# Moving the last query block's product with V behind the second logits, in the last of four attention segments

## Chip, cores and metric

The kernel runs on one core of a Trainium2 chip. The metric is the device time of one execution in microseconds (us); lower is better. Every run told of here was at a granted TensorE clock of 1.0. Executions of one kernel lie within about 0.5 us of each other.

## The reference

A residual block in two halves: attention with a compressive memory, then a gated MLP with a spatial mix. Only the first half matters here. For each of 32 heads of 32 columns, in four segments of 512 tokens:

```python
for s in range(4):
    qs, ks, vs = q[:, :, s], k[:, :, s], v[:, :, s]
    logits = einsum('bhqd,bhkd->bhqk', qs, ks) * scale + mask      # causal
    p = softmax(logits)
    a_dot = einsum('bhqk,bhkd->bhqd', p, vs)                       # "the product with V"
    a_mem = (phi(qs) @ M) / (phi(qs) @ z + 1e-06)                  # memory of earlier segments
    outs.append(g * a_mem + (1 - g) * a_dot)
    M = M + phi(ks)^T @ vs                                         # state update
    z = z + sum(phi(ks))
```

After the last segment nobody reads M and z, so the kernel leaves that state update out.

## The kernel before

The kernel records instructions for each engine in program order, and a tracker adds the semaphore waits. It tracks SBUF in cells of 32 bytes and PSUM in whole banks (2 KiB). A wait means: this bank or cell is still being read or written by another engine.

PSUM has 8 banks. Banks 0 to 3 hold the logits of four heads, 4 and 5 the product with V (`PVA`), and 6 and 7 rotate for projections and state. A *group* `n` is four heads of one segment: 8 groups a segment, 32 in all, and the last segment has groups 24 to 31.

```python
def logits(n, rnd):                       # rnd 0, 1, 2: first, second, third logits
    parts = {0: ((0, 0, 512),), 1: ((1, 0, 384), (3, 384, 128)), 2: ((2, 0, 256),)}[rnd]
    wid = (512, 512, 256)[rnd]
    e = E[n % 2][rnd]
    for j, o, w in parts:
        for i in range(4):                # four heads, four 32-row tiles of the array
            pe.matmul(PS[:, i, o:o + w], qk[...], qk[...], ..., tile_position=(32 * i, 0))
    if rnd == 2 and n >= NQ:
        mem(n)                            # phi(q) @ M, reads MZB[:, c]
    act.activation(e[:, :, 0:wid], PS[:, 0:4, 0:wid], ACTF.Exp, scale=float(SCALE))
    # ... causal mask on GpSimd; for rnd 2 the memory's normalisation

def pv(n):                                # product with V: 4 query blocks, 40 matmuls
    c = n % NQ
    for cq in range(4):
        for j in range(cq + 1):
            rnd, o = {0: (0, cq * 128), 1: (1, cq * 128 - 128), 2: (2, cq * 128 - 256), 3: (1, 384)}[j]
            for i in range(4):
                pe.matmul(PVA[:, cq, i, :], E[n % 2][rnd][:, i, o:o + 128], V[:, j, 4 * c + i, 0:33],
                          start=(cq % 2 == 0 and j == 0 and i == 0), stop=False, ...)
    norm(n)                               # VectorE: divide by the row sums, add the memory part

def state(n):
    s, c = divmod(n, NQ)
    if s == NSEG - 1:
        return                            # nothing in the last segment
    b = next_bank()
    for tcl in range(4):
        pe.matmul(PS[:, b, 0:132], PK[n % 3][:, tcl, :], V[:, tcl, 4 * c:4 * c + 4, 0:33], ...)
    # ... VectorE: MSUM += bank, then MZB[:, c] = MSUM * mask
```

The order within a group:

```python
    logits(n, 0)
    fill(f1)                  # K projection of group n + 1: 8 matmuls of 512 columns
    if n > 0:
        pv(n - 1)
    logits(n, 1)
    if n > 0:
        state(n - 1)
    bg_pop()
    fill(f2)                  # Q projection of group n + 1: 8 matmuls of 512 columns
    logits(n, 2)
    # ... fill(f3), fill(f4): V or output projections
```

All three rounds of logits write the same four banks. So the second logits must wait for the exp of the first, and the third for the exp of the second. What stands between them on TensorE decides whether it stops.

The softmax here doesn't subtract the row's maximum and nothing guards it: scores larger than these inputs give would overflow.

Of the kernel before, what the change touches and what calls it, by code (L numbers as in the profile page):

```python
# [14 lines left out]
NSEG = 4  # L15
# [242 lines left out]
def bass_sequential_preLN__memory_aug_infini_attn__mixer_gmlp__prompt_kernel(  # L258
# [123 lines left out]
    def x_load(tc):  # L382
        sp.dma_start(XCH[tc % 4][:], x2d[tc * 128:(tc + 1) * 128, :])

    def wcols(ap, lo, hi):
        return ap[:, lo:hi].rearrange("(c p) n -> p c n", p=128)
# [29 lines left out]
    def mask_g():  # L416
        dve.tensor_copy(MASKG[:, :, :, 0:32],
                        GS[:].rearrange("p (c i) -> p c i", i=4).unsqueeze(3).to_broadcast([128, NQ, 4, 32]))
        for i in range(4):
            dve.tensor_single_scalar(MASKG[:, :, i, 0:32], MASKG[:, :, i, 0:32], BLK[:, i:i + 1], ALU.mult)  # L420
        for c in range(NQ):
            dve.tensor_copy(MASKG[:, c, :, 32], BLK[:])
# [24 lines left out]
    def to_T(dst, tcl, src):  # L447
        sp.dma_start_transpose(dst[:, :, tcl * 128:(tcl + 1) * 128], src[:])
# [40 lines left out]
    def phi_exp(n):  # L489
        q, p, e = phi_views(n)  # L490
        act.activation(e, q, ACTF.Exp)

    def phi_max(n):
        q, p, e = phi_views(n)
        dve.tensor_single_scalar(p, q, 1.0, ALU.add)
        dve.tensor_single_scalar(e, e, 1.0, ALU.min)
        dve.tensor_tensor(p, p, e, ALU.max)
        if n // NQ < NSEG - 1:
            sp.dma_start_transpose(PK[n % 3][:], PQK[n % 2][:, 1, :])


    def logits(n, rnd):
        qk = QK[n % 2]
# [5 lines that stand above are left out]
                pe.matmul(PS[:, i, o:o + w], qk[32 * i:32 * (i + 1), 1, j * 128:(j + 1) * 128],  # L509
                          qk[32 * i:32 * (i + 1), 0, j * 128:512], start=True, stop=True,  # L510
                          tile_position=(32 * i, 0))
        if rnd == 2 and n >= NQ:
            mem(n)
        act.activation(e[:, :, 0:wid], PS[:, 0:4, 0:wid], ACTF.Exp, scale=float(SCALE))
        for j, o, w in parts:
            d = e[:, :, o:o + 128]
            pool.affine_select(out=d, in_=d, pattern=[[0, 4], [1, 128]], compare_op=ALU.is_ge, fill=0.0,
                               base=0, channel_multiplier=-1)
        if rnd == 2 and n >= NQ:
            mem_norm(n)  # L520

    def pv(n):
        c = n % NQ
        for cq in range(4):
            for j in range(cq + 1):
                rnd, o = {0: (0, cq * 128), 1: (1, cq * 128 - 128), 2: (2, cq * 128 - 256), 3: (1, 384)}[j]
                for i in range(4):
                    pe.matmul(PVA[:, cq, i, :], E[n % 2][rnd][:, i, o:o + 128], V[:, j, 4 * c + i, 0:33],
                              start=(cq % 2 == 0 and j == 0 and i == 0), stop=False, skip_group_check=True)
        norm(n)  # L530

    def mem(n):
        c = n % NQ
        for cq in range(4):
            pe.matmul(PS[:, cq, 256:388], PQK[n % 2][:, 0, cq * 128:(cq + 1) * 128], MZB[:, c, :, 0:33],
                      start=True, stop=True)

    def mem_norm(n):
        om = PS[:, 0:4, 256:388].rearrange("p q (i d) -> p q i d", d=33)
        dve.tensor_single_scalar(RDM[:], om[:, :, :, 32], float(MEM_EPS), ALU.add)  # L540
        dve.reciprocal(RDM[:], RDM[:])
        dve.tensor_tensor(TM[n % 2][:], om[:, :, :, 0:32], RDM[:].unsqueeze(3).to_broadcast([128, 4, 4, 32]), ALU.mult)

    def norm(n):
        s, c = divmod(n, NQ)
        ot = OTOK[s % 2][:, :, c * 128:(c + 1) * 128].rearrange("p q (i d) -> p q i d", d=32)
        dve.reciprocal(RD[:], PVA[:, :, :, 32])
        dve.tensor_tensor(RD[:], RD[:], OMG[:, c:c + 1, :].to_broadcast([128, 4, 4]), ALU.mult)
        rb = RD[:].unsqueeze(3).to_broadcast([128, 4, 4, 32])
        if s == 0:  # L550
            dve.tensor_tensor(ot, PVA[:, :, :, 0:32], rb, ALU.mult)
        else:
            dve.tensor_tensor(TA[:], PVA[:, :, :, 0:32], rb, ALU.mult)
            dve.tensor_tensor(ot, TA[:], TM[n % 2][:], ALU.add)
        if c == NQ - 1:
            for tcl in range(4):
                to_T(OT, tcl, OTOK[s % 2][:, tcl, :])
# [4 lines that stand above are left out]
            return  # L562
        b = next_bank()
        for tcl in range(4):
            pe.matmul(PS[:, b, 0:132], PK[n % 3][:, tcl, :], V[:, tcl, 4 * c:4 * c + 4, 0:33],
                      start=(tcl == 0), stop=(tcl == 3))
        if s == 0:
            dve.tensor_copy(MSUM[:, c, :], PS[:, b, 0:132])
        else:
            dve.tensor_tensor(MSUM[:, c, :], MSUM[:, c, :], PS[:, b, 0:132], ALU.add)  # L570
        dve.tensor_tensor(MZB[:, c, :, 0:33], MSUM[:, c, :].rearrange("p (i d) -> p i d", d=33), MASKG[:, c, :, :],
                          ALU.mult)


    def xr_load(tc):
        sp.dma_start(XR[tc % 2][:], x2d[tc * 128:(tc + 1) * 128, :])
# [15 lines left out]
    def ln_tasks(src, dst, tcl):  # L592
        lnq[0].append((src, dst, tcl))

    def bg_pop():
        if lnq[2]:
            src, dst, tcl, k = lnq[2].pop(0)
            to_T(dst, tcl, ln_apply(src, k))
        if lnq[1]:
            it = lnq[1].pop(0)  # L600
            ln_rstd(it[3])
            lnq[2].append(it)
        if lnq[0]:
            it = lnq[0].pop(0)
            lnq[1].append(it + (ln_stats(it[0]),))
# [68 lines left out]
    def z2_gelu(k, tc, src):  # L674
        act.activation(Z2[:, tc, k * 448:(k + 1) * 448], src, ACTF.Gelu_apprx_tanh)
        zs.append((k, tc))
# [16 lines left out]
    for n in range(LAST + 1):  # L693
        s, c = divmod(n, NQ)
        f1, f2, f3, f4 = [], [], [], []
        if n < LAST:
            f1, f2 = [("qk", n + 1, 1)], [("qk", n + 1, 0)]
        if s == 0:
            f3 = [("v", 0, c, 1)] if c < 4 else [("v", 1, c - 4, 0)]
        elif s < NSEG - 1:  # L700
            if c < 2:
                f3, f4 = [("v", s, 2 * c, 1)], [("v", s, 2 * c + 1, 1)]
            elif c < 6:
                f3, f4 = [("wo", s - 1, c - 2, 0)], [("wo", s - 1, c - 2, 1)]
            else:
                f3, f4 = [("v", s + 1, 2 * (c - 6), 0)], [("v", s + 1, 2 * (c - 6) + 1, 0)]
        elif c < 2:
            f3, f4 = [("v", s, 2 * c, 1)], [("v", s, 2 * c + 1, 1)]
        elif c < 6:
            f3, f4 = [("wo", s - 1, c - 2, 0)], [("wo", s - 1, c - 2, 1)]  # L710
        elif c == 6:
            f3, f4 = [("z2", 0, 4, 0)], [("z2", 0, 5, 1)]
        else:
            f1, f2 = [("z2", 0, 6, 2)], [("z2", 0, 7, 3)]
            f3, f4 = [("z2", 0, 0)], [("z2", 0, 1)]

        def fill(lst):
            for u in lst:
                {"v": proj_v, "wo": wo, "qk": proj_qk, "z2": z2_group}[u[0]](*u[1:])

        if s < NSEG - 1 and c < 4:
            ln_tasks(XCH[c], XNT[(s + 1) % 2], c)
        if s < NSEG - 2 and c >= 4:
            x_load(4 * (s + 2) + c - 4)
        if s > 0 and c == 1:
            xr_load(4 * (s - 1))

        logits(n, 0)
        fill(f1)
        if n > 0:  # L730
            pv(n - 1)
        logits(n, 1)
        if n > 0:
            state(n - 1)
        bg_pop()
        fill(f2)
        logits(n, 2)
        if n == 0:
            mask_g()
        if n < LAST:  # L740
            phi_exp(n + 1)
        while n == LAST and staged:
            z2_gelu(*staged.pop(0))
        fill(f3)
        if n < LAST:
            phi_max(n + 1)
        bg_pop()
        fill(f4)
        bg_pop()
        if n == 1:  # L750
            sp.dma_start(WO[:], wcols(A_wo, 0, D))
        if n in (24, 26):
            win_load((n - 24) // 2)
    pv(LAST)
    xr_load(4 * (NSEG - 1))

# [98 lines left out]
```

## Time and profile before

| | before |
|---|---|
| time, median of 3 runs | 805.35 us (805.32 to 805.37) |
| span of the profiled run | 803.7 us |
| TensorE busy | 795.0 us, 99% |
| TensorE waits in the last segment | 1.3 us in the list, 7 times |

The profile page of the kernel before, its busy times and its chain of waits (the work that ended last, traced back):

```profile
span 803.7 us, 12539 instructions
...
PE 795.0 (99%) x5407; PEld 384.0 (48%) x5407; DVE 367.8 (46%) x756; ACT 302.7 (38%) x360; POOL 120.5 (15%) x234
...
PE 94%; DVE 2%; ACT 2%; DMA 0%; issue 0%
```

TensorE (PE) is the engine to relieve. Everything else is under half busy. With the same instructions, a gain can come only from TensorE's gaps.

The timeline of the kernel before, part of group 28 (start, duration, engine, operation with output and inputs, count, and in brackets the idle time in front and what ended it; TensorE's rows, with ScalarE's row of the second exp put among them, and other rows left out):

```profile
283.84 0.40 PE L209 MATMUL ps<-qk_102 32*128 32x512 bf16 x4
284.17 1.90 PE L209 MATMUL ps<-xnT_78,wk 128*128 128x512 bf16 x8
...
286.82 0.25 PE L209 MATMUL ps<-v,e_110 128*128 128x33 bf16 x4
287.01 0.40 PE L209 MATMUL ps<-qk_102 32*128 32x384 bf16 x8
287.34 1.90 PE L209 MATMUL ps<-xnT_78,wq 128*128 128x512 bf16 x8
...
287.46 1.88 ACT L209 ACTIVATE e_113<-ps 128x2048 bf16<-128x2048 f32 x1 [0.75 <-PE ps L209]
...
289.39 0.29 PE L209 MATMUL ps<-qk_102 32*128 32x256 bf16 x4 [0.15 <-ACT e_113 L209]
```

Read it from the end. The third logits (289.39) follow the exp of the second (287.46 + 1.88 = 289.34) by 0.05 us. The Q projection started at 287.34, and eight such matmuls are done well before. The bracket says 0.15 us, but the starts say more: from this projection to the third logits is 2.05 us, while the K projection hands over to the product with V after 1.74 us. (That hand-over has no change of tile shape. With one it takes about 1.83 us without a stop, as is worked out below, so the stop is 0.22 us and not the whole difference.) A matmul's end is modelled and overlaps the next start, so the bracket counts a stop too small.

The list of waits of TensorE, kernel before, from 240 to 320 us (total us, times, longest):

```profile
PE ps L209 <- ACT e_113 L209: 0.8, 4, 0.4
PE ps L209 <- ACT e_110 L209: 0.5, 3, 0.2
```

Seven stops, all on the second exp. And the chain of waits in order of time, kernel before, 276 to 310 us:

```profile
279.83 7.61 PE ps L209 x84
287.43 0.02 issue
287.46 1.89 ACT e_113 L209
289.34 0.05 issue
289.39 7.59 PE ps L209 x84
```

Once in each group the critical path leaves TensorE for ScalarE's exp and comes back.

### The profile page before, as it was taken

What the parts mean: (1) busy time and instruction counts of PE and PEld (TensorE: products, weight loads), DVE (VectorE), ACT (ScalarE), POOL (GpSimd) and SP (SyncE); (2) the same over time, 40 slices, a digit from 0 to 9 for tenths busy, and PEclk for the clock granted to TensorE, in tenths of its full rate; (3) what the DMA queues carried; (4) which work ended last, traced back from release to release, by engine and by line L of the source; (5) the groups of instructions that cost most, each with busy time, mean ns of one, the idle gap of its engine ahead of it and who ended that gap; (6) DMA issues with size and microseconds to landing.
All of it is one profiled execution on the core that took longest, in us unless ns stands there. A gap on an engine that the chain in (4) does not pass through costs nothing.

```text
span 803.7 us, 12539 instructions
## 1 busy us (share of the span) xinstructions
PE 795.0 (99%) x5407; PEld 384.0 (48%) x5407; DVE 367.8 (46%) x756; ACT 302.7 (38%) x360; POOL 120.5 (15%) x234
## 2 busy tenths in 40 slices
PE   8999999999999999999999999999999999999998
PEld 4445544455554445455544444444444444444444
DVE  4653688669854675844563000054234324423332
ACT  3888876887787666133333333100000000000000
POOL 2342333233322331100131000000000000000000
PEclk9999999999999999999999999999999999999999
DMA  9682544454425323621116000550270044011002
GB/s 296 157 172 60 92 80 119 80 99 81 93 47 126 113 54 68 189 60 53 53 53 131 1 1 0 193 115 1 79 138 1 26 106 85 1 59 53 1 7 86
DMA packets 125992, 64.79 MB, mean 81 GB/s; under 512 B 94832, under 2 KB 114928, under 8 KB 125936
## 3 DMA queue, kind: packets, MB, share of 16 engines
q1 hardware_dynamic: 125936, 63.99, 33.9%
q8 instruction: 42, 0.69, 0.3%
q14 instruction: 14, 0.11, 0.1%
HBM read 32.51 MB, written 8.39 MB: 51 GB/s over the span
## 4 chain that ended last, share of the span: by engine, by line
PE 94%; DVE 2%; ACT 2%; DMA 0%; issue 0%
PE ps L209 94%; ACT e_113 L209 1%; ACT e_110 L209 1%; DMA xch_97<-in_A_x_dram 0%; DVE stats_61 L209 0%; DVE stats_62 L209 0%; ACT e_109 L209 0%; DVE stats_59 L209 0%; DVE ta L209 0%; DVE otok_120 L209 0%; DVE hch_86 L209 0%; DVE stats_60 L209 0%; DVE pqk_104 L209 0%; DVE lno_90 L209 0%; DVE rd L209 0%
## 5 line engine op out<-in xcount | busy, mean ns | idle before, releaser
L209 PE MATMUL ps<-w_out,yT 128*128 128x512 bf16 (+1 forms) x462 | 97.4, 373 | 0.0
L209 PE MATMUL ps<-wspT_127,z_124 128*128 128x512 bf16 x448 | 97.0, 379 | 0.0
L209 PE MATMUL ps<-wspT_126,z_124 128*128 128x512 bf16 x448 | 97.0, 379 | 0.0
L209 PEld LDWEIGHTS ps<-w_out,yT 128*128 128x128 bf16 x462 | 45.2, 98 | 51.7
L209 PEld LDWEIGHTS ps<-wspT_126,z_124 128*128 128x128 bf16 x448 | 43.8, 98 | 52.9
L209 PEld LDWEIGHTS ps<-wspT_127,z_124 128*128 128x128 bf16 x448 | 43.8, 98 | 52.9
L209 DVE TENSOR_TENSOR tmpg_133<-ps,brow_131 128x512 f32<-128x512 f32 x14 | 9.7, 690 | 116.1 <-DMA brow_131<-in_B_b_sp_dram 95.7
L209 ACT ACTIVATE z_124<-ps 128x448 bf16<-128x448 f32 x60 | 32.4, 542 | 69.5 <-PE ps L209 69.5
L209 PE MATMUL ps<-wo,oT 128*128 128x512 bf16 x256 | 57.9, 379 | 0.0
L209 ACT ACTIVATE z1T<-ps 128x512 bf16<-128x512 f32 x56 | 33.4, 597 | 63.3 <-PE ps L209 63.3
L209 DVE BATCH_NORM_STATS2 zst<-z_124 128x6 f32<-128x448 bf16 x64 | 38.9, 619 | 30.1 <-ACT z_124 L209 30.1
L209 PEld LDWEIGHTS ps<-wo,oT 128*128 128x128 bf16 x256 | 24.5, 98 | 27.2
L209 ACT ACTIVATE e_109<-ps 128x2048 bf16<-128x2048 f32 x16 | 30.0, 1875 | 11.8 <-PE ps L209 11.8
L209 ACT ACTIVATE e_112<-ps 128x2048 bf16<-128x2048 f32 x16 | 30.0, 1874 | 11.8 <-PE ps L209 11.8
L209 ACT ACTIVATE e_113<-ps 128x2048 bf16<-128x2048 f32 x16 | 30.0, 1877 | 10.8 <-PE ps L209 10.8
L209 ACT ACTIVATE e_110<-ps 128x2048 bf16<-128x2048 f32 x16 | 30.0, 1877 | 9.9 <-PE ps L209 9.9
L209 PE MATMUL ps<-xnT_78,wk 128*128 128x512 bf16 x128 | 30.4, 380 | 0.0
L209 PE MATMUL ps<-xnT_77,wk 128*128 128x512 bf16 x128 | 30.4, 380 | 0.0
L209 PE MATMUL ps<-xnT_78,wq 128*128 128x512 bf16 x128 | 30.3, 379 | 0.0
L209 PE MATMUL ps<-xnT_77,wq 128*128 128x512 bf16 x128 | 30.2, 379 | 0.0
L209 DVE RECIPROCAL rd<-ps 128x16 f32<-128x16 f32 x32 | 7.8, 244 | 48.8 <-PE ps L209 48.8
L209 POOL TENSOR_SCALAR_AFFINE_SELECT e_113<-e_113 128x512 bf16<-128x512 bf16 x32 | 20.2, 653 | 38.7 <-ACT e_113 L209 38.7
(230 smaller groups left out, 1204.0 us busy)
## 6 DMA issues: line engine op xcount, KB each, us to landing
w_out<-in_B_w_out_dram SPq DMA_DIRECT2D x1, 3584.0 KB, 12.6
wo<-in_A_wo_dram SPq DMA_DIRECT2D x1, 2048.0 KB, 10.1
xr_84<-in_A_x_dram SPq DMA_DIRECT2D x8, 256.0 KB, 3.7
xr_85<-in_A_x_dram SPq DMA_DIRECT2D x8, 256.0 KB, 3.8
win_121<-in_B_w_in_dram SPq DMA_DIRECT2D x2, 896.0 KB, 5.1
wk<-in_A_wk_dram SPq DMA_DIRECT2D x1, 1536.0 KB, 10.4
wq<-in_A_wq_dram SPq DMA_DIRECT2D x1, 1536.0 KB, 14.1
out_dram<-hch_86 SPq DMA_DIRECT2D x6, 256.0 KB, 2.8
```

What stands on the lines that cost most here:

```text
L209: ins = getattr(e, op.name)(*op.args, **op.kw)
```

## The change

Its intent: in the last segment, put some of TensorE's own work between the second logits and the third, where earlier segments have the state update. The last of the four query blocks of the product with V (16 of 40 matmuls) goes there. The first three stay where they were.

```diff
-    def pv(n):
+    def pv(n, cqs=range(4)):
         c = n % NQ
-        for cq in range(4):
+        for cq in cqs:
             ...
-        norm(n)
+        if 3 in cqs:
+            norm(n)
@@
         logits(n, 0)
         fill(f1)
         if n > 0:
-            pv(n - 1)
+            pv(n - 1, range(3) if s == NSEG - 1 else range(4))
         logits(n, 1)
+        if s == NSEG - 1:
+            pv(n - 1, (3,))
         if n > 0:
             state(n - 1)
```

No instruction is added or dropped. Only TensorE's order changes, in eight groups.

## The prediction

> **What bounds the kernel.** TensorE: the page gives it 795.0 of 803.7 us busy at full clock, and the chain of waits is 94% matmuls. All its waits together are 5.7 us, most of them in the start-up.
>
> **Where the change acts.** The timeline of the last segment shows one repeated stop, before the third logits. They overwrite the PSUM banks that the exp of the second logits reads. That exp starts 0.45 us after the second logits start, takes 1.88, and the third logits start 0.05 after its end: 2.38 us after the second logits (287.01 to 289.39). TensorE has only the second logits (0.33) and one projection to put between. Earlier segments have four state matmuls (0.24) there too, and no wait shows. The last segment has no state update, except in its first group (third logits at 241.62, no idle).
>
> The seven later groups stop. Start to start, projection to third logits is 2.05 us. Unhindered it would be 1.84: eight matmuls at 213 ns (1.706) plus the 0.137 that the same transition takes after sixteen output-projection matmuls (3.55 - 3.413). Six groups lose 0.21 us each. The last, whose filler is 448 columns wide (1.49 + 0.14 = 1.63), loses 0.42. Sum: 6 x 0.21 + 0.42 = 1.7 us. The list of waits, which counts from a matmul's modelled end, has 6 x 0.15 + 0.37 = 1.27 for the same stops.
>
> **What the change does.** No instruction is added or removed. Sixteen matmuls of the fourth query block (25 ns each, 0.40 us in the timeline) move behind the second logits, which with their exp start 0.40 earlier. In six groups TensorE then has 0.33 + 0.40 + 1.84 = 2.57 us of work against the 2.38 us exp chain: the stop disappears with 0.19 to spare. The last group has 2.36 against 2.38: about 0.02 remains. The first group gains nothing.
>
> Switches between row-tiled logits and full-array matmuls cost about 0.1 us each and stay as many. (The Trainium skill, TensorEngine Tiling, Key Properties: changing the tiling mode drains the engine; the gaps of 0.09 and 0.12 us around the second logits agree.) The moved matmuls keep the 25 ns step, which the skill's TensorE: Matmul & The Clock Gate ("Wait — 56ns, not 53.3ns?") gives as the floor; the trace agrees.
>
> **Can the exp start earlier?** ScalarE idles 0.64 to 0.75 us before it in the six groups, 0.54 in the last, all over 0.40. The first exp ends 0.8 us before the second logits in the six groups; in the last at 304.94 against 305.47, so 0.13 is left, enough for 0.05 of signalling. VectorE's normalisation comes about 0.33 later relative to the logits, with some 2 us of idle after it: free.
>
> All 1.7 us lies on the critical path: afterwards TensorE runs 493 us without a wait, so the rest moves forward.
>
> **Prediction.** 805.35 - 1.65 = 803.7 us; range 803.2 to 804.6. Faster by over 2% 0.005, within 2% 0.99, slower by over 2% 0.005.
>
> **What would show it.** The seven waits of the third logits on the second exp vanish (at most a few hundredths in the last group); each of the six groups' period falls from 9.56 to about 9.35 us; the tail after attention keeps its length.
>
> **What would make it wrong.** An exposed weight load or a second drain at the moved matmuls (0.1 us per group: gain about 1 us); ScalarE's queue holding the exp in the last group; a new wait of the first logits; a DMA in the tail that doesn't move with TensorE.

## The result, and the profile after

| | before | after |
|---|---|---|
| time, median of 4 runs each, same rounds | 805.34 us | 803.69 us (803.45 to 803.78) |
| ratio, 95% interval | | 0.9979 (0.9962 to 0.9997) |
| span of the profiled run | 803.7 us | 801.9 us |
| TensorE waits in the list, 240 to 320 us | 7 | none |
| period of groups 25 to 30 | 9.55 us | 9.33 us |
| period of group 31 | 8.91 us | 8.51 us |
| from the last third logits to the end | 495.8 us | 495.8 us |

Ratios are the mean time of one kernel's runs over that of the other's of the same rounds, so not quite the ratio of the medians quoted. A period is the time from the third logits of the preceding group to those of the group named, read from the timeline.

The profile page after, the same lines:

```profile
span 801.9 us, 12469 instructions
...
PE 791.5 (99%) x5337; PEld 384.1 (48%) x5407; DVE 368.0 (46%) x756; ACT 303.1 (38%) x360; POOL 123.1 (15%) x234
...
PE 94%; DVE 4%; issue 1%; ACT 1%; DMA 0%
```

The trace after has 70 fewer matmul records than before, though the program has as many (the weight loads still number 5407). Some matmul records were lost. So the fall of TensorE's busy time, 3.5 us, must not be read as a saving; the starts must be.

The timeline after, the same part of group 28:

```profile
282.96 0.40 PE L209 MATMUL ps<-qk_102 32*128 32x512 bf16 x4
283.29 1.90 PE L209 MATMUL ps<-xnT_78,wk 128*128 128x512 bf16 x8
...
285.72 0.40 PE L209 MATMUL ps<-qk_102 32*128 32x384 bf16 x8
286.05 0.27 PE L209 MATMUL ps<-v,e_109 128*128 128x33 bf16 x4
...
286.17 1.88 ACT L209 ACTIVATE e_113<-ps 128x2048 bf16<-128x2048 f32 x1 [0.35 <-PE ps L209]
...
286.68 1.67 PE L209 MATMUL ps<-xnT_78,wq 128*128 128x512 bf16 x7
...
288.29 0.29 PE L209 MATMUL ps<-qk_102 32*128 32x256 bf16 x4
```

The second logits and their exp come sooner after the first logits: 2.76 us instead of 3.17. The exp ends at 288.05, and the third logits start at 288.29, 0.24 us after that. They no longer wait for it. (In the timeline the projection shows seven matmuls because its first record was lost; its weight loads start at 286.44.)

In the last group, 31, a remnant is left:

```profile
304.20 1.88 ACT L209 ACTIVATE e_113<-ps 128x2048 bf16<-128x2048 f32 x1
...
306.13 0.29 PE L209 MATMUL ps<-qk_102 32*128 32x256 bf16 x4
```

The third logits start 0.05 us after the end of this exp (304.20 + 1.88 = 306.08), as they did at every stop before. Here the stop is longer than the 0.40 us moved. What remains is small: with the shortened exp of the experiments below, which leaves no stop, the same group takes 8.48 us instead of 8.51.

The chain of waits after, in order of time, 276 to 310 us:

```profile
277.34 9.28 PE ps L209 x91
286.62 0.06 issue
286.68 9.27 PE ps L209 x91
295.95 0.06 issue
296.01 13.99 PE ps L209 x132
```

ScalarE is off the chain in this stretch. (The two "issue" entries stand where the first record of a projection was lost.) TensorE's list of waits from 240 to 320 us is empty. The remnant in group 31 is too short to show in either.

Where the time came from: the third logits of group 24 start at 241.62 us in both profiles, those of group 31 at 307.85 before and 306.13 after. So 1.72 us were won in seven groups, and the tail passed them on whole.

### The profile page after: what moved, and what is told of

Same layout as the page of the kernel before. It is cut to its first block, busy times and chain, and to the rows that moved or that the text cites. A ratio compares the mean times of both kernels' runs of the same rounds, so it can differ in the third digit from the quotient of the medians.

```text
span 801.9 us, 12469 instructions
## 1 busy us (share of the span) xinstructions
PE 791.5 (99%) x5337; PEld 384.1 (48%) x5407; DVE 368.0 (46%) x756; ACT 303.1 (38%) x360; POOL 123.1 (15%) x234
## 3 DMA queue, kind: packets, MB, share of 16 engines
HBM read 32.51 MB, written 8.39 MB: 51 GB/s over the span
## 4 chain that ended last, share of the span: by engine, by line
PE 94%; DVE 4%; issue 1%; ACT 1%; DMA 0%
PE ps L209 94%; DVE stats_61 L209 0%; DVE stats_62 L209 0%; DVE ta L209 0%; DMA xch_97<-in_A_x_dram 0%; ACT e_110 L209 0%; ACT e_109 L209 0%; DVE rd L209 0%; DVE stats_59 L209 0%; DVE pqk_104 L209 0%; DVE otok_119 L209 0%; DVE otok_120 L209 0%; DVE hch_87 L209 0%; DVE hch_86 L209 0%; DVE stats_60 L209 0%
## 5 line engine op out<-in xcount | busy, mean ns | idle before, releaser
L209 PE MATMUL ps<-xnT_77,wq 128*128 128x512 bf16 x113 | 27.0, 379 | 0.9 <-issue 0.2
L209 PE MATMUL ps<-xnT_78,wq 128*128 128x512 bf16 x112 | 26.8, 379 | 0.9
```

The lines of the kernel that those rows point to most:

```text
L209: ins = getattr(e, op.name)(*op.args, **op.kw)
```

## The experiments

The theory to test, **A**: the gain is the stop of the third logits on the second exp, covered by the moved work. Per group it is the smaller of the stop and the work moved, as long as nothing else is delayed. Rivals: **B**, the new order runs faster on TensorE by itself (cheaper switches between tile shapes, earlier weight loads); **C**, an extra switch costs something that the gain hid.

All kernels were timed in five rounds, with nine runs of before on the same chip. "Gain" is before's median minus the kernel's.

| kernel | before | this | gain | ratio (95%) |
|---|---|---|---|---|
| ctl_early_segments | 805.46 | 809.49 | -4.03 | 1.0049 (1.0037 to 1.0062) |
| filler_before | 805.46 | 805.48 | -0.02 | 1.0000 (0.9988 to 1.0013) |
| filler_after | 805.46 | 805.29 | 0.17 | 0.9997 (0.9985 to 1.0010) |
| short_exp_before | 805.46 | 803.71 | 1.75 | 0.9978 (0.9964 to 0.9991) |
| short_exp_after | 805.42 | 803.79 | 1.63 | 0.9981 (0.9967 to 0.9994) |
| ctl_early_padded | 805.42 | 807.36 | -1.94 | 1.0024 (1.0012 to 1.0037) |
| move_8 | 805.42 | 804.04 | 1.38 | 0.9984 (0.9971 to 0.9996) |
| move_all | 805.42 | 806.24 | -0.82 | 1.0010 (0.9998 to 1.0023) |
| move_4 | 805.41 | 804.83 | 0.58 | 0.9993 (0.9981 to 1.0006) |
| move_28 | 805.41 | 804.29 | 1.12 | 0.9986 (0.9973 to 0.9998) |
| first_group | 805.41 | 803.68 | 1.73 | 0.9978 (0.9964 to 0.9991) |
| first_group_padded | 805.41 | 803.19 | 2.22 | 0.9973 (0.9960 to 0.9985) |

The start-up differs by some tenths of a us from run to run: in the kernels whose start-up is unchanged, the third logits of group 0 start anywhere from 27.05 to 27.70 us in the profiles. Periods within one trace are free of that, so they are given beside the times. Where the interval of a ratio includes 1 (both fillers, move_4, move_all), the time alone does not tell the kernel from before, and the periods carry the argument.

### Useless work in the stop: filler_before and filler_after

The four state matmuls are issued in the last segment too, into a rotating bank that nobody reads. This goes into the kernel before and into the kernel after.

```diff
     def state(n):
         s, c = divmod(n, NQ)
-        if s == NSEG - 1:
-            return
         b = next_bank()
         for tcl in range(4):
             pe.matmul(PS[:, b, 0:132], PK[n % 3][:, tcl, :], V[:, tcl, 4 * c:4 * c + 4, 0:33],
                       start=(tcl == 0), stop=(tcl == 3))
+        if s == NSEG - 1:
+            return
```

Expected of filler_before:

> Kernel before, but in the last segment the four state matmuls are issued too, into a spare PSUM bank that nobody reads (0.24 us of useless TensorE work in each of seven groups). Theory A: six stops of 0.21 us hide nearly all of it and the last one all, so +6 x 0.03 = 0.2: 805.5 us, and the wait of the third logits is gone in the six groups. Theory B (order, not idle time): the work adds up, +7 x 0.24 = 1.7: 807.0 us.

Expected of filler_after:

> Kernel after with the same useless four matmuls in seven groups. Theory A: no stop is left to hide them, +7 x 0.24 = 1.7: 805.35 us against 803.7 of after. If a stop that the profile doesn't show remained, it would cost less.

Measured: 805.48 us against 805.46 in the old order, and 805.29 in the new. The same 28 useless matmuls cost 0.02 us in the old order (0.1 by the periods). In the new they cost 1.6 us (805.29 against 803.69, the latter from other rounds). Within these rounds, the two kernels with filler differ by 0.19 us, where the kernels without it differ by 1.65. In filler_before's trace the waits of the third logits are gone from the list and the period is 9.57 us, as in earlier segments. So the old order had idle time of just about this size at this place, and the change uses it up. Rival B, in which the work would have added up to 807.0, falls.

### Removing the cause, not the order: short_exp_before and short_exp_after

The second exp covers 384 of 512 columns. The result is wrong: one block of the probabilities is stale. (The comparison with the reference still passed its tolerance, so that comparison is no proof of this part.)

```diff
-        act.activation(e[:, :, 0:wid], PS[:, 0:4, 0:wid], ACTF.Exp, scale=float(SCALE))
+        ew = 384 if rnd == 1 and n >= NQ * (NSEG - 1) else wid
+        act.activation(e[:, :, 0:ew], PS[:, 0:4, 0:ew], ACTF.Exp, scale=float(SCALE))
```

> Kernel before in its old order, but the second exp of each group of the last segment covers 384 of 512 columns (wrong result on purpose): 1.88 us become about 1.45. Theory A: the stop goes without any reordering, 805.35 - 1.65 = 803.7 us, as after. Theory B: no reordering, no gain, 805.3 us.

> Kernel after with the shortened second exp in the last segment (wrong result on purpose). Theory A: the stop that the short exp removes is already gone, so no further gain: 803.65 us, as after and as the shortened exp in the old order (803.7). If the reordering and the exp acted on different things, their gains would add: 802.0 us.

Measured: 803.71 us in the old order, 803.79 in the new. The shortened exp takes 1.45 us. The timeline of short_exp_before, group 28:

```profile
286.17 0.40 PE L209 MATMUL ps<-qk 32*128 32x384 bf16 x8
...
286.62 1.45 ACT L209 ACTIVATE e<-ps 128x1536 bf16<-128x1536 f32 x1 [0.75 <-PE ps L209]
...
288.33 0.29 PE L209 MATMUL ps<-qk 32*128 32x256 bf16 x4
```

The exp ends at 288.07 and the third logits follow 0.26 us later without a wait. The period is 9.33 us, that of the kernel after. Taking 0.43 us off the exp does in the old order what the reordering does, and the two don't add. They act on the same stop. (In short_exp_after, group 25 takes 9.48 us instead of 9.33. Its trace shows the same late read of a PSUM bank that is met in move_28 below.)

### How much to move: move_4, move_8, move_28, move_all

The query blocks, or part of the last one, are moved in the last segment only. For move_8:

```diff
-            pv(n - 1, range(3) if s == NSEG - 1 else range(4))
+            pv(n - 1, range(4), range(2) if s == NSEG - 1 else range(4))   # key blocks of query block 3
         logits(n, 1)
         if s == NSEG - 1:
-            pv(n - 1, (3,))
+            pv(n - 1, (3,), range(2, 4))
```

The third argument, which `pv` gets in these kernels, chooses the key blocks of query block 3. move_4 uses `range(3)` and `range(3, 4)`; move_28 moves query blocks 2 and 3; move_all moves all four.

> Only the last 4 matmuls move (0.10 us), the smallest step. Theory A: every one of the seven stops is longer than that, so 7 x 0.10 = 0.7 us, 804.7 us against 805.4 of before, with the seven waits of the third logits still in the trace but shorter. In proportion to 1.65 us for 16: 0.41 us, 805.0 us.

> Only the last 8 of the 16 matmuls of the fourth query block move (0.20 us of work). Theory A (gain per group is the smaller of the stop and the work moved): 6 x 0.20 + 0.20 = 1.4 us, 803.95 us. A gain in proportion to the number moved would be 0.83 us: 804.5 us.

> The third and the fourth query block move (28 matmuls, 0.70 us). Theory A: the second logits can come 0.79 us earlier in five groups, so there the gain stays 0.21 and no more; in the first two they are held by the first exp at 0.63 (loss 0.07 each), in the last at 0.48 (loss 0.22 of 0.42). 6 x 0.21 + 0.42 - 0.14 - 0.22 = 1.3 us: 804.1 us. Sixteen matmuls are then near the best number.

> In the last segment all 40 matmuls of the product with V (1.0 us) move behind the second logits. Theory A: now the second logits reach their own limit, the end of the first exp, which comes 0.79 us (0.63 in the first two groups, 0.48 in the last) before they could start. The stop moves from the third logits to the second: 0.21 us in five groups (no net gain), 0.37 in each of the first two (-0.37 and -0.16 net), 0.52 in the last (-0.10 net), so about 806.0 us, with waits of the second logits on the first exp in all eight groups. If covering were all that counts (more moved never hurts): 803.7 us.

Gain against the number of matmuls moved. The column "by periods" is the sum of the periods of groups 24 to 31 before, 75.79 us, minus the same sum of the kernel:

| moved | theory A, as expected | gain measured | by periods |
|---|---|---|---|
| 4 | 0.7 | 0.58 | 0.69 |
| 8 | 1.4 | 1.38 | 1.40 |
| 16 (the change) | 1.65 | 1.65 | 1.71 |
| 28 | 1.3 | 1.12 | 1.01 |
| 40 | -0.6 | -0.82 | -0.81 |

The gain doubles from 4 to 8, grows little to 16 (mostly in the last group, whose stop is the longest: 8.71 us with 8 moved, 8.51 with 16), and then falls below nothing. A gain in proportion to the number moved (0.41 and 0.83 at 4 and 8) does not fit the periods: move_4 gains 0.10 us in each of the seven groups (9.55 to 9.45, and 8.91 to 8.81), exactly the work moved. One expectation failed. I had written that move_4's trace would still list seven shorter waits. It lists one, of 0.3 us in the last group. The other six are stops of about 0.12 us. Of these the modelled end of the matmul before leaves 0.05 us of idle time in the trace, and the list leaves out so short a time: no entry or bracket shown here is under 0.15.

Beyond 16, other limits are met. The timeline of move_all, group 28:

```profile
284.90 1.90 PE L209 MATMUL ps<-xnT,wk 128*128 128x512 bf16 x8
...
285.02 1.88 ACT L209 ACTIVATE e<-ps 128x2048 bf16<-128x2048 f32 x1 [2.25 <-PE ps L209]
...
286.95 0.40 PE L209 MATMUL ps<-qk 32*128 32x384 bf16 x8 [0.15 <-ACT e L209]
```

Now the second logits stop, 0.05 us after the end of the first exp (285.02 + 1.88 = 286.90). In this group the period is 9.56 us, what it was before. The stop has only changed places. Groups 27, 29 and 30 fare alike; groups 24, 25, 26 and 31 lose 0.37, 0.15, 0.15 and 0.10 us. Two sizes were off. First, I had put the tighter limit of 0.63 us on two groups. A V projection's eviction on ScalarE holds up the first exp in a third one, group 26, too: its period is 9.70 in move_all instead of 9.55. Second, in move_28, group 25 has 9.68 us instead of about 9.4, for a reason that the theory lacked. It is seen at the end of group 24:

```profile
240.90 1.11 DVE L209 TENSOR_TENSOR otok<-ta,tm 128x512 bf16<-128x512 f32 x1
...
241.53 0.29 PE L209 MATMUL ps<-qk 32*128 32x256 bf16 x4
241.75 0.41 PE L209 MATMUL ps<-mzb,pqk 128*128 128x132 bf16 x4
241.93 0.28 DVE L209 TENSOR_TENSOR msum<-msum,ps 128x132 f32<-128x132 f32 x1
...
242.26 1.04 PE L209 MATMUL ps<-wv,xnT 128*128 128x512 bf16 x4
```

The V projection follows the memory matmuls by 0.51 us instead of 0.25 (241.84 to 242.09 in the kernel before). It starts 0.05 us after VectorE's `msum` instruction has read the bank. (The count of a view's last row, here x4, is cut off by the end of the window asked for.) The later the last query block, the later VectorE's normalisation, and the state's PSUM bank is read only behind it. That same delay is the main character of the next experiment.

### The same reordering where there is no stop: ctl_early_segments and ctl_early_padded

The reordering goes into segments 0 to 2 only (23 groups), and the last segment keeps the old order.

```diff
-            pv(n - 1)
+            pv(n - 1, range(3) if s < NSEG - 1 else range(4))
         logits(n, 1)
+        if n > 0 and s < NSEG - 1:
+            pv(n - 1, (3,))
```

> The same reordering in segments 0 to 2 only (23 groups), none in the last. There the state matmuls already stand behind the second logits and no stop shows. Theory A (the moved matmuls cover the rest of the exp that the third logits wait for): nothing to cover, 805.35 us within 0.2. Theory B (the new order by itself runs faster on TensorE, by cheaper switches or earlier weight loads, 0.22 us per group): 805.35 - 23 x 0.22 = 800.3 us. Theory C (an extra switch at the moved matmuls costs 0.1 us that the gain hid): 807.6 us.

Measured: 809.49 us, 4.0 us slower. None of the three theories had foreseen this. Rival B is refuted once more, as nothing was gained in 23 groups. But A's "nothing happens" failed as well, and C's constant cost per group does not fit the trace: in segments 1 and 2 every second group keeps its period of 9.57 us, and the others go to 10.1 or 10.2. The list of waits of TensorE in ctl_early_segments has a line that before has not:

```profile
PE ps L209 <- DVE mzb L209: 3.9, 8, 0.6
```

Eight waits, 3.9 us: that is nearly all of the loss. The timeline of ctl_early_segments around one of them:

```profile
195.54 0.69 DVE L209 TENSOR_TENSOR otok<-ta,tm 128x512 bf16<-128x512 f32 x1
...
196.08 0.29 PE L209 MATMUL ps<-qk 32*128 32x256 bf16 x4
196.15 0.28 DVE L209 TENSOR_TENSOR msum<-msum,ps 128x132 f32<-128x132 f32 x1
...
196.47 0.41 DVE L209 TENSOR_TENSOR mzb<-msum,maskg 128x132 bf16<-128x132 f32 x1
...
196.94 0.41 PE L209 MATMUL ps<-mzb,pqk 128*128 128x132 bf16 x4 [0.58 <-DVE mzb L209]
```

The memory matmuls of this group wait for the state update of the *previous* group, which VectorE runs behind the normalisation (`otok` is its last step). The reordering delays the normalisation. But one group's update and the next group's memory matmuls touch different columns of `MZB`, so why wait? `MZB` has 4 x 34 bf16 columns per group of heads, 272 bytes, which is eight and a half of the tracker's 32-byte cells. Two neighbours share a cell, and only every second pair does: hence every second group. The next kernel tests this.

```diff
-    MZB = cb("mzb", [128, NQ, 4, 34], BF16)
+    MZB = cb("mzb", [128, NQ, 4, 36], BF16)
```

> The reordering in segments 0 to 2 again, which cost 4.0 us, with the masked memory tile MZB padded from 34 to 36 columns per head, so that the 272 bytes of one group of heads become 288 and two groups no longer share a 32-byte cell of the dependence tracker. Theory D (the loss is a false dependence: the memory matmuls of every second group wait for the neighbour's state update, which VectorE does behind the normalisation that the reordering delays): the eight waits vanish and the time is 805.4 us within 0.3. Theory E (VectorE is simply too late, or TensorE pays an extra switch): it stays at 809.4 us.

Measured: 807.36 us. It recovers 2.1 of the 4.0 us, where theory D said all and theory E nothing. The trace says which part of D held. The eight waits on `mzb` are gone, and 14 of the 16 groups of segments 1 and 2 run at 9.56 or 9.57 us, the unhindered period. In the two remaining ones (10.75 us each) a new wait stands. The timeline of ctl_early_padded:

```profile
126.79 0.41 PE L209 MATMUL ps<-mzb,pqk 128*128 128x132 bf16 x4
126.99 0.94 DVE L209 TENSOR_TENSOR otok<-ta,tm 128x512 bf16<-128x512 f32 x1
...
127.85 0.28 DVE L209 TENSOR_TENSOR msum<-msum,ps 128x132 f32<-128x132 f32 x1
...
128.19 2.98 PE L209 MATMUL ps<-wo,oT 128*128 128x512 bf16 x13 [0.99 <-DVE msum L209]
```

Here VectorE is busy with layer-norm statistics and comes later still. The output projection wants the bank that holds the state product, and waits 0.99 us until VectorE has read it. Two such waits are 2.0 us in the list, which is the rest of the loss: here VectorE is simply too late, as the first half of theory E said. (The padding alone also shortens four groups that were late in before, by 0.44 us in all; see first_group_padded. Against a padded before, which was not run, the two groups would have lost 2 x (10.75 - 9.59) = 2.3 us, an estimate from the periods.) So the reordering itself, with its switches, is free in 14 groups out of 16: C falls. It is harmful wherever a state update stands behind the normalisation. This is shown by the traces of the two kernels. What is left open is a version without the second wait, which was not tried.

### Two tries at a better version: first_group and first_group_padded

In after's trace the very first group still stops on exps, 0.60 us before the second logits and 0.15 before the third. The edit to the kernel after:

```diff
     v_quarter(3, 0)
-    v_quarter(3, 1)
-    phi_exp(0)
-    phi_max(0)
@@
         if s == NSEG - 1:
             pv(n - 1, (3,))
+        if n == 0:
+            phi_exp(0)
+            phi_max(0)
+            v_quarter(3, 1)
```

> Kernel after, with the same idea applied to the very first group, where the second logits wait 0.60 us and the third 0.15 us for exps (in after's trace too). A quarter of a V projection (0.9 us) and the exp of the feature map move from in front of the first logits to behind the second. ScalarE then reaches the first exp about 1.0 us earlier and the quarter covers the second exp. Expected 0.4 to 0.6 us below after: 803.2 us. If ScalarE alone sets the pace there, nothing is gained: 803.7 us.

> The kernel of the run before this one, with the masked memory tile padded to 36 columns as well. In before, three of every eight memory matmul groups of segments 1 and 2 start 0.32 to 0.34 us after the third logits and not 0.22, five times in all, which the false dependence explains: 5 x 0.10 = 0.5 us less if so, 802.7 us; if not, the same as without the padding, 803.2 us.

Measured: first_group 803.68 us, nothing gained over after (gain 1.73 against 1.65, from other rounds). It is not that ScalarE alone sets the pace: the third logits of group 0 did come earlier. Their times, 26.76 us and 27.20 in after, contain the scatter of the start-up. Counted from the start of the last transposes of the start-up (14.73 and 14.51) it is 12.03 us instead of 12.70, and 12.70 is what all twelve kernels with an unchanged start-up have. So 0.67 us were won. But group 2's period went from 7.60 to 8.21 us. TensorE's list of waits in first_group has this line:

```profile
PE ps L209 <- DVE msum L209: 0.5, 1, 0.5
```

VectorE's moved feature map pushed back the 3.3 us in which it builds the mask (29.16 to 32.51 us in this trace), and the state bank was read late once more. The 0.67 us won were lost again but for 0.06 (8.21 - 7.60 = 0.61), most of it in this one wait. Building the mask earlier would be the next try; it was not run.

first_group_padded, with `MZB` padded on top, took 803.19 us, 0.49 less than first_group in the same rounds. The expectation's count was wrong: before's timeline has four late memory groups (0.32 to 0.34 us behind the third logits and not 0.22), not five. The periods that follow, 9.66 to 9.69 us in first_group, are 9.57 with the padding, some 0.11 us less each. So 0.44 us of the 0.49 are seen at that place, and the cause is the false dependence that the padding takes away. This is the fastest kernel measured here; its edit in the first group contributes next to nothing. The padding on top of after alone was not run.

## Why the prediction was right

Predicted 803.7 us (803.2 to 804.6) and within 2% at 0.99; measured 803.69. That even the last digits agree is luck: the periods give 1.72 us won where 1.65 was forecast, and the four runs of after spread over 0.33 us. The mechanism was right point by point, with one term slightly off:

- **What bounds the kernel, and where.** Right. All 1.72 us came from the seven third logits named, none from elsewhere.
- **The size of the stop, 0.21 us in six groups and 0.42 in the last.** The gain measured is 0.22 (periods 9.55 to 9.33) and 0.40 (8.91 to 8.51), in the last group the work moved and not the whole stop, as the prediction said. The list of waits, 1.27 us, would have underestimated the gain; the start-to-start sum did not. One term was slightly off: the 1.84 us of an unhindered hand-over rested on a pace of 512-column matmuls that no trace here shows. In a dense stretch of before's trace (500 to 600 us) 464 of them start, 0.2158 us apart. From the start of sixteen of them to the row-tiled logits behind them are 3.55 us, so the change adds 0.10 (3.55 - 16 x 0.2158). Eight and a change are 1.83 us, and the stop is 0.22.
- **The exp can start 0.40 us earlier.** Right: ScalarE's idle time in front of it fell from 0.75 to 0.35 us in group 28, and the exp was never late. The margin of the first exp was put at 0.8 us for all six groups. That was too much for groups 25 and 26, but it did not matter at 0.40. move_28 and move_all show where it does.
- **Switches.** Right: no extra cost. (The Trainium skill, "TensorEngine Tiling (Array Packing)", Key Properties, says that changing the tiling mode drains the engine. The 0.09 and 0.10 us added at changes into row-tiled logits agree with it, and the number of changes stays.)
- **VectorE's later normalisation is free.** Right, but only where it was claimed. In the last segment no state update stands behind it after the first group. In the first, the delay cost nothing in after, but 0.15 us in short_exp_after and about 0.28 in move_28 (both in the period of group 25). In the earlier segments the same delay costs 4.0 us. The prediction didn't see that this is why the change stops at the last segment.
- **GpSimd.** Not predicted and without consequence: its two masks after the second exp take 1.54 us instead of 1.22 in group 28, as they now overlap the end of the normalisation. The Trainium skill, "SBUF — State Buffer", two separate sides, says that a VectorE instruction with two SBUF inputs and a GpSimd instruction that reads SBUF exclude each other for a whole instruction. This agrees with it: `otok` reads two SBUF tiles until 288.57, and the masks, which start at 288.12, take 0.32 us longer (0.45 if they were held to its end). In move_28 the masks start first, at 240.83, and both lose: `otok` takes 1.11 us and not 0.69, the two masks 1.67 and not 1.22.
- **The tail moves forward whole.** Right: 495.8 us in both.

## What to carry to other kernels

Compute what one reordering can win as the smaller of the stop and the work put into it, from start to start; a list of waits hides some 0.07 us of each stop behind modelled ends, and leaves out what is then too short. Then ask what the moved work releases and who queues behind that. Here 0.4 us of delay was free in one segment and cost 4.0 us in the earlier ones, because the next PSUM bank or a shared dependence cell waited behind the same VectorE work. Move no more than the stop needs: past it the stop only changes places.

## What the Trainium skill lacked or had wrong

- "TensorE: Matmul & The Clock Gate", Back-to-back issue gap, gives 131 ns per 512-column matmul as the sustained pace of a real kernel with weight loads, and calls about 216 ns over-counted. Here 464 of them start in 100 us of a dense stretch, each with its own weight load: 216 ns. The figure that this section calls isolated is the one that held; the same page, under "Wait — 56ns, not 53.3ns?", gives it (215.7 ns) as measured back to back.
- "TensorEngine Tiling (Array Packing)", Key Properties, names the drain at a change of tiling mode but gives no cost. Here the last of four 33-column matmuls, at a step of 25 ns, should be followed 0.10 us after the first (286.82 us); the row-tiled logits started at 287.01, so 0.09 us were added. From 512-column matmuls into row-tiled ones it was 0.10 us (3.55 - 16 x 0.2158). That all of this is the drain is not shown.
- No page that I read says what a list of waits loses when matmul ends are modelled (it would belong to "Perfetto Trace Analysis"): of seven stops in move_4, the six of about 0.12 us left no entry, and the last, of about 0.32, one of 0.3.
